# Expert tiles of a routed feed-forward kernel: rows loaded by a transposing DMA, output scatters ahead of the others, longer modelled waits

## The chip, the cores and the metric

The kernel runs on one core of a Trainium2 chip. The metric is the device time of one execution in microseconds (us). Engines are named as in the profile: PE (TensorE matmul), PEld (its weight load), DVE (VectorE), ACT (ScalarE), POOL (GpSimd) and SP (SyncE, which here only issues DMAs).

## The reference

A gated recurrence over four sequences feeds a router with eight experts; each token goes through one expert's two-layer network.

```python
# x, f_logit: (4, 5056, 256); 20224 tokens in all
sig = 1.0 / (1.0 + np.exp(-f_logit))
f = lower_bound + (1.0 - lower_bound) * sig
i = 1.0 - f
for t in range(S):
    h = f[:, t] * h + i[:, t] * x[:, t]
    y[:, t] = h
x = y.reshape(20224, 256)
xn = x / (np.linalg.norm(x, axis=-1, keepdims=True) + 1e-06)
en = expert_emb / (np.linalg.norm(expert_emb, axis=-1, keepdims=True) + 1e-06)
logits = xn @ en.T / tau
expert_idx = np.argmax(logits, axis=1)
probs = softmax(logits)
gate_w = probs[np.arange(N), expert_idx]
for e in range(8):                       # w1: (8, 256, 1024), w2: (8, 1024, 256)
    mask = expert_idx == e
    out[mask] = gate_w[mask, None] * (np.maximum(x[mask] @ w1[e], 0.0) @ w2[e])
```

## The kernel before

The program has two kinds of work. **Chunks**: the 20224 tokens are taken in 40 chunks of 512. For each chunk SP loads `fin` and `xin` (512 KB each, three buffers), PE transposes them (`F_`, line 546, and `X_`, line 575), ACT and DVE make the gates, DVE runs the recurrence as a scan (line 599), PE transposes the result back (`Y_`, line 618) and ACT writes it in bf16 to `Yt`, a row of 256 values per token with the gate weight and the token's number behind them. `route_` and `gate_` work out, for groups of two chunks, each token's expert and its slot `sli`; then POOL scatters the rows, 128 to a DMA, to their slots in `XsScratch`, a table in device memory with a region for each expert (line 832, "an Xs scatter" below; 158 of them, 16 to a batch of four chunks).

**Tiles**: 256 rows of one expert are a tile; there are 86. `tile_` loads the rows to `xsb` (line 996, 132 KB, six buffers), PE transposes them in four pieces into a PSUM bank (`yt`, line 1013), DVE copies them to `ys` (line 1021, two buffers), PE multiplies by the first weights (`mm1`, line 1036, 16 matmuls), ACT and DVE take turns in the four evictions to `hT` (lines 1051 and 1056), PE multiplies by the second weights (`mm2`, line 1067, 16 matmuls), ACT and DVE scale the two halves into `osb` (lines 1081 and 1085, four buffers), and POOL scatters both to the output rows (line 1091, "an output scatter" below, 172 of them). The scale and the output row's number are read from `xsb` too, so a buffer of `xsb` is held until the output scatters that read it are done. For the first 70 tiles `mm1` takes turns in banks 5 and 6 and the transposed rows take bank 5 as well; later tiles have banks of their own.

Which tiles may run is settled by `update_` at eight points, when enough rows of an expert are known; a tile's load waits for the Xs scatters of all groups up to that point.

The order of instructions on each engine is fixed before the run. `Prog.schedule` plays the program through with a cost for each operation, lets each engine take, of what is ready, the operation with the lowest `prio`, and writes the order down; on the chip every engine works through its list in that order, with semaphore waits where data come from elsewhere. `LAT` is the time that the planner adds between an operation and one on another engine that needs it; a DMA takes `DMA_FIX` ns and its bytes over `DMA_RATE`. A tile's `prio` is set in `put`, an Xs scatter's is the number of its chunk:

```python
pr.prio = groups[g][-1] + 3.0 + 0.5 * (j - avail.index((u, g)))
```

Of the kernel before, what the change touches and what calls it, by code (L numbers as in the profile page):

```python
# [7 lines left out]
P = 128  # L8
F32 = mybir.dt.float32
BF16 = mybir.dt.bfloat16  # L10
I32 = mybir.dt.int32
# [5 lines left out]
class Op:  # L17
    __slots__ = (
        "eng", "fn", "deps", "order", "dma", "val", "know", "used", "cost", "nbytes", "prio",
        "idx", "start", "end", "tag",  # L20
    )


class Prog:
# [2 lines left out]

    LAT = 90  # L30
    DMA_FIX = 1900
    DMA_RATE = 300.0

    def __init__(self):
        self.ops = []
# [55 lines left out]
    def schedule(self):  # L91
# [19 lines left out]
        while True:  # L111
# [28 lines left out]
            for q, hard in succ[id(o)]:  # L140
                t = (o.end + self.LAT) if hard else free[e]
                if q.eng == e and o.dma is None and hard:
# [75 lines left out]
def bass_hgrn_recurrence__then__cosine_router_kernel(  # L218
# [12 lines left out]
    E, _, Fdim = moe_w1.shape  # L231
    assert D == 2 * P and Fdim == 8 * P and E == 8 and N % 256 == 0
    DT = D // P
# [4 lines left out]
    NCH = (N + CH - 1) // CH  # L238
    T = 256
    CAP = N + T  # L240
    RW = 264
    NT = N // T + E - 1
    NULLROW = E * CAP
    CB = CAP // T
# [6 lines left out]
    Xs = nc.dram_tensor("XsScratch", [E * CAP + T, RW // 2], I32, kind="Internal").ap()  # L251

    pr = Prog()
    op = pr.op

    with ExitStack() as es:

        def sb(name, shape, dt=F32):
            return es.enter_context(nc.sbuf_tensor(name, shape, dt))
# [7 lines left out]
        identb = sb("identb", [P, P], BF16)  # L267
# [31 lines left out]
        Yt = [sb(f"Yt{q}", [P, 16, RW], BF16) for q in range(NY)]  # L299
# [24 lines left out]
        dac = sb("dac", [P, 2])  # L324
        tbl = [sb(f"tbl{q}", [P, 2], I32) for q in range(NU)]
        nrow = sb("nrow", [P, E], I32)
        NX = 6
        xsb = [sb(f"xsb{q}", [P, 2, RW], BF16) for q in range(NX)]
        ys = [sb(f"ys{q}", [P, DT, T], BF16) for q in range(2)]
        NHT = 2  # L330
        hT = [sb(f"hT{q}", [P, FT, T], BF16) for q in range(NHT)]
        NO = 4
        osb = [sb(f"osb{q}", [P, 2, D]) for q in range(NO)]

        bank = [ps(f"bank{q}", [P, 512]) for q in range(8)]
# [3 lines left out]
        def pool(fn, cost=400, **k):  # L339
            return op("pool", fn, cost, **k)  # L340

        def dve(fn, n, fast=False, **k):
            return op("dve", fn, 130 + n * (0.55 if fast else 1.04), **k)
# [4 lines left out]
        def pe(fn, cost, **k):  # L348
            return op("pe", fn, cost, **k)
# [42 lines left out]
        def iota(dst, pattern, base=0, mult=0, w=()):  # L392
# [7 lines left out]
                out=ident[:], in_=ident[:], compare_op=ALU.not_equal, fill=1.0,  # L400
                base=0, pattern=[[-1, P]], channel_multiplier=1,
            ),
            r=["ident"], w=["ident"],
# [16 lines left out]
                out=scr[:], in_=scr[:], compare_op=ALU.is_ge, fill=1.0,  # L420
                base=0, pattern=[[-1, P]], channel_multiplier=1,
            ),
            r=["scr"], w=["scr"],
# [8 lines left out]
        for q in range(R2):  # L432
            pool(lambda e, q=q: e.memset(exb[q][:], 1e-9), w=[("exb", q)])
        for q in range(NY):
            pool(lambda e, q=q: e.memset(Yt[q][:, :, 260:264], 0.0), w=[("ytz", q)])
        pool(lambda e: e.memset(oh[0][:, 64:72], 0.0), w=[("oh", 0)])

        def late_constants():
# [545 lines left out]
                    )  # L984


        evr = {}

        def tile_(j, u, g, phb, pob, ysb):

            qx, qy, qh, qo = j % NX, j % 2, j % NHT, j % NO
            last = u == len(ups) - 1

            def ld(e):
                r = e.value_load(tbl[u][j : j + 1, 0:1], min_val=0, max_val=NULLROW)
                return e.dma_start(
                    xsb[qx][:].bitcast(I32),
                    Xs[bass.ds(r, T), :].rearrange("(p s) r -> p s r", s=2),
                )

            rd = [("tbl", u), ("nt", 0), ("nt", 1)]
            rd += [("Xs", g_) for g_ in range(g + 1)]
            if last:
                rd += ["nul"]
            op("sp", ld, 700, r=rd, w=[("xsb", qx)], dma=f"xs{qx}", nbytes=135168)

            ysT = bank[ysb][:, 0:256].bitcast(BF16)

            def yt(e):
                o = ysT.rearrange("p (k s c) -> p k s c", k=2, s=2)  # L1010
                for s in range(2):
                    for kt in range(DT):
                        i = e.transpose(  # L1013
                            o[:, kt, s, :], xsb[qx][:, s, kt * P : (kt + 1) * P], identb[:]
                        )
                return i

            pr.prio -= YBOOST
            pe(yt, 310, r=[("xsb", qx), "identb"], x=[ysb])
            dve(  # L1020
                lambda e: e.tensor_copy(ys[qy][:].rearrange("p k c -> p (k c)"), ysT),  # L1021
                512, True, x=[ysb], w=[("ys", qy)],
            )
            pr.prio += YBOOST
            prev = None
            for m in range(4):
                pb = phb[m % len(phb)]

                def mm1(e, m=m, pb=pb):
                    if m == 0:  # L1030
                        evr[j] = e.value_load(
                            tbl[u][j : j + 1, 1:2], min_val=0, max_val=(E - 1) * WE
                        )
                    for fi in range(2):
                        for kt in range(DT):
                            i = e.matmul(  # L1036
                                bank[pb][:, fi * T : (fi + 1) * T],
                                wb[0][:, bass.ds(evr[j] + (kt * Fdim + (2 * m + fi) * P), P)],
                                ys[qy][:, kt, :],
                                start=(kt == 0), stop=(kt == DT - 1),  # L1040
                            )
                    return i

                prev = pe(
                    mm1, 490, r=[("ys", qy), ("tbl", u)] + [("w", i) for i in range(2 * E)],
                    x=[pb], order=[prev],
                )
                o = hT[qh][:, 2 * m : 2 * m + 2, :].rearrange("p f c -> p (f c)")
                if m % 2 == 0:
                    act(  # L1050
                        lambda e, o=o, pb=pb: e.activation(o, bank[pb][:], AF.Relu), 512,  # L1051
                        x=[pb], w=[("hT", qh, m)],
                    )
                else:
                    dve(
                        lambda e, o=o, pb=pb: e.tensor_scalar(  # L1056
                            o, bank[pb][:], 0.0, None, op0=ALU.max
                        ),
                        512, x=[pb], w=[("hT", qh, m)],
                    )  # L1060
            po = [bank[pob[0]][:, 0:D], bank[pob[1]][:, D : 2 * D]]
            one = pob[0] == pob[1]
            for m in range(4):
                def mm2(e, m=m):
                    for kf in (2 * m, 2 * m + 1):
                        for s in range(2):
                            i = e.matmul(  # L1067
                                po[s], hT[qh][:, kf, s * P : (s + 1) * P],
                                wb[1][:, bass.ds(evr[j] + kf * D, D)],
                                start=(kf == 0 and not (one and s)), stop=(kf == FT - 1),  # L1070
                                skip_group_check=one,
                            )
                    return i

                pe(
                    mm2, 480, r=[("hT", qh, m)] + [("w", i) for i in range(2 * E)],
                    x=sorted(set(pob)), order=[prev],
                )
            gx = [xsb[qx][:].bitcast(F32)[:, s, 128:129] for s in range(2)]
            act(  # L1080
                lambda e: e.activation(osb[qo][:, 0, :], po[0], AF.Copy, scale=gx[0]), 256, 1,  # L1081
                x=[pob[0]], r=[("xsb", qx)], w=[("osb", qo, 0)],
            )
            dve(
                lambda e: e.tensor_scalar(osb[qo][:, 1, :], po[1], gx[1], None, op0=ALU.mult),  # L1085
                340, x=[pob[1]], r=[("xsb", qx)], w=[("osb", qo, 1)],
            )
            for s in range(2):
                op(
                    "pool",  # L1090
                    lambda e, s=s: e.indirect_dma_start(  # L1091
                        out=out[:, :],
                        out_offset=bass.IndirectOffsetOnAxis(
                            ap=xsb[qx][:].bitcast(I32)[:, s, 129:130], axis=0
                        ),
                        in_=osb[qo][:, s, :],
                        in_offset=None,
                        bounds_check=N - 1,
                        oob_is_err=False,
                    ),  # L1100
                    1280, r=[("osb", qo, s), ("xsb", qx)], w=[("out", j, s)], dma=f"od{qo}_{s}",
                    nbytes=131072,
                )


# [3 lines left out]
        for u, g in enumerate(ups):  # L1109
            tok = sum(nof(c) for gg in range(g + 1) for c in groups[gg])  # L1110
            k = max(0, -(-(tok - E * (T - 1)) // T)) if u < len(ups) - 1 else NT
# [3 lines left out]
        YBOOST = 1.5  # L1115
# [30 lines left out]
        for j in range(NT):  # L1146
# [3 lines left out]
           r=["nul"])  # L1150
# [38 lines left out]
```

## Time and profile before

| | |
|---|---|
| median of 3 runs | 775.52 us (771.86 to 776.4) |
| the profiled execution | 781.91 us |
| its span, first to last instruction | 780.0 us |
| PE busy | 591.7 us, 76% of the span |
| DVE busy | 399.0 us |
| ACT busy | 342.8 us |
| POOL busy | 387.7 us |
[...]

The spans and durations below are of the profiled execution. Up to 174 us there are chunks alone; from there to about 640 us chunks and tiles share the engines; then tiles alone. Matmul records give the issue times; ends are modelled, so the count of matmuls in a stretch is a better measure of PE's progress than its busy time, above all where the granted clock is low.

### The profile page before, as it was taken

The page shows a single profiled execution, that of the slowest core. Times are in us where ns is not written, and L with a number is a line of the kernel's source. Part 1 is how long each engine was busy: PE and PEld are TensorE (multiplying, and loading weights), DVE is VectorE, ACT ScalarE, POOL GpSimd, SP SyncE. Part 2 cuts the span into 40 slices and gives each one's busy share as a digit, 9 for nine tenths or more (in the row PEclk, how much of TensorE's full clock was granted, in tenths as well). Part 3 has the DMA queues.
Part 4 walks back from the last instruction along what each step waited for, and adds up shares of the span by engine and source line. Part 5 has one row for each costly group of instructions (what it writes and reads, how often), then busy time and mean ns, then how long its engine had stood idle before and what let it go on. Part 6 is the DMA issues. An engine that isn't in the chain of part 4 may idle for free.

```text
span 780.0 us, 14923 instructions
## 1 busy us (share of the span) xinstructions
PE 591.7 (76%) x4656; PEld 430.5 (55%) x4656; DVE 399.0 (51%) x923; ACT 342.8 (44%) x574; POOL 387.7 (50%) x410
## 2 busy tenths in 40 slices
PE   5876676658868996879984698289848866999994
PEld 4543444436556764656763476167535544677773
DVE  4876556616435655354572465157705534445552
ACT  6976556534324623443542265064523522333431
POOL 4267757564644346563347335723572544335443
PEclk9998869769979999999997699579957977999997
DMA  9998886933313424332334244233311113223210
GB/s 277 284 276 209 223 168 195 222 119 106 100 59 104 153 69 134 98 111 84 121 109 136 72 151 127 80 129 123 106 60 56 63 42 117 83 84 99 65 58 1
DMA packets 80534, 95.04 MB, mean 122 GB/s; under 512 B 9089, under 2 KB 70797, under 8 KB 80464
## 3 DMA queue, kind: packets, MB, share of 16 engines
q1 hardware_dynamic: 56592, 54.15, 23.5%
q0 software_dynamic: 23872, 39.94, 18.5%
q8 instruction: 46, 0.75, 0.4%
q14 instruction: 24, 0.20, 0.1%
HBM read 69.83 MB, written 34.44 MB: 134 GB/s over the span
## 4 chain that ended last, share of the span: by engine, by line
PE 61%; another core or an unknown queue 11%; DVE 8%; issue 7%; ACT 7%; POOL 4%; DMA 1%; POOLq 0%; ACTq 0%; DVEq 0%
PE bank L1036 23%; PE bank L1067 19%; PE bank L618 4%; PE bank L546 4%; PE bank L575 3%; PE bank L666 3%; PE bank L1013 3%; POOL XsScratch L832 3%; DVE hb L599 2%; ACT hT L1051 2%; POOL nr L775 2%; DVE hT L1056 2%; DVE nx L583 1%; ACT th L554 1%
## 5 line engine op out<-in xcount | busy, mean ns | idle before, releaser
L1091 POOL DMA_INDIRECT out_dram<-osb,xsb x172 | 171.8, 999 | 257.8 <-DVE osb L1085 162.4
L1036 PE MATMUL bank<-ys,w1b 128*128 128x256 bf16 x1376 | 217.1, 290 | 57.3 <-issue 26.5
L1036 PEld LDWEIGHTS bank<-ys,w1b 128*128 x1376 | 135.5, 99 | 130.8 <-issue 92.0
L832 POOL DMA_INDIRECT XsScratch<-Yt,sli x158 | 164.0, 1038 | 82.9 <-issue 45.4
L1067 PE MATMUL bank<-w2b,hT 128*128 x1376 | 186.1, 282 | 21.2 <-DVE hT L1056 20.8
L1056 DVE TENSOR_SCALAR hT<-bank 128x512 bf16<-128x512 f32 x172 | 118.2, 687 | 90.7 <-PE bank L1036 54.7
L1067 PEld LDWEIGHTS bank<-w2b,hT 128*128 128x128 bf16 x1376 | 131.4, 101 | 43.6 <-issue 24.2
L1051 ACT ACTIVATE hT<-bank 128x512 bf16<-128x512 f32 x172 | 102.4, 596 | 114.5 <-PE bank L1036 87.9
L1081 ACT ACTIVATE osb<-bank,xsb 128x256 f32<-128x256 f32 x86 | 40.7, 473 | 174.2 <-PE bank L1067 104.9
L599 DVE TENSOR_TENSOR_SCAN hb<-fg,hb,nx 128x512 f32<-128x512 f32 (+4 forms) x78 | 97.1, 1245 | 1.4
L1085 DVE TENSOR_SCALAR osb<-bank,xsb 128x256 f32<-128x256 f32 x86 | 41.4, 482 | 103.5 <-ACT osb L1081 82.1
L618 PE MATMUL bank<-ident,hb 128*128 128x128 f32 x316 | 57.3, 311 | 33.4 <-issue 15.2
L546 PE MATMUL bank<-ident,fin 128*128 128x128 f32 x316 | 58.0, 314 | 23.8 <-ACT th L554 10.3
L618 PEld LDWEIGHTS bank<-ident,hb 128*128 128x128 f32 x316 | 40.4, 158 | 54.9 <-issue 33.2
L583 DVE SCALAR_TENSOR_TENSOR nx<-fg,bank 128x512 f32<-128x512 f32 (+1 forms) x80 | 53.9, 673 | 31.6 <-PE bank L575 8.5
L1021 DVE COPY ys<-bank 128x512 bf16<-128x512 bf16 x86 | 36.3, 422 | 64.5 <-issue 16.3
L626 ACT ACTIVATE Yt<-bank 128x512 bf16<-128x512 f32 x79 | 46.6, 590 | 47.9 <-remote 29.2
L560 ACT ACTIVATE fg<-th,cs 128x512 f32<-128x512 f32 (+1 forms) x80 | 64.6, 807 | 1.9
L575 PE MATMUL bank<-ident,xin 128*128 128x128 f32 x316 | 56.6, 308 | 8.9 <-DVE nx L583 8.0
L554 ACT ACTIVATE th<-bank 128x512 f32<-128x512 f32 (+1 forms) x80 | 47.1, 589 | 35.1 <-PE bank L546 20.6
L546 PEld LDWEIGHTS bank<-ident,fin 128*128 128x128 f32 x316 | 42.7, 162 | 28.7 <-ACT th L554 13.9
L611 ACT ACTIVATE sq<-hb 128x1024 f32<-128x1024 f32 (+1 forms) x40 | 41.6, 1041 | 22.4 <-DVE hb L599 21.7
(113 smaller groups left out, 419.7 us busy)
## 6 DMA issues: line engine op xcount, KB each, us to landing
fin<-in_f_logit_dram SPq DMA_DIRECT2D x39, 512.0 KB
xin<-in_x_dram SPq DMA_DIRECT2D x39, 512.0 KB
xsb<-XsScratch SPq DMA_DIRECT2D x86, 132.0 KB
w1b<-in_moe_w_dram POOLq DMA_DIRECT2D x8, 512.0 KB, 7.4
w2b<-in_moe_w_dram POOLq DMA_DIRECT2D x8, 512.0 KB, 7.7
out_dram<-osb,xsb POOLq DMA_INDIRECT x172
XsScratch<-Yt,sli POOLq DMA_INDIRECT x158
XsScratch<-nulr SPq DMA_DIRECT2D x8, 132.0 KB
```

Source lines behind the costliest of these rows:

```text
L546: i = e.transpose(bank[BF][:, b * P : (b + 1) * P], fin[q][:, b, dh * P : (dh + 1) * P], ident[:],)
L560: lambda e, dh=dh: e.activation(fg[c % 2][:, dh, 0:n], th[dh][:, 0:n], AF.Identity, bias=cs[:, dh, 0:1], scale=cs[:, dh, 1:2],),
L575: i = e.transpose(bank[BX][:, b * P : (b + 1) * P], xin[q][:, b, dh * P : (dh + 1) * P], ident[:],)
L583: lambda e, dh=dh: e.scalar_tensor_tensor(out=nx[c % 2][:, dh, 0:n], in0=fg[c % 2][:, dh, 0:n], scalar=1.0, in1=bank[BX][:, 0:n], op0=ALU. ...
L599: lambda e, dh=dh, s0=s0, s1=s1, init=init: e.tensor_tensor_scan(hb[c % NH][:, dh, s0:s1], fg[c % 2][:, dh, s0:s1], nx[c % 2][:, dh, s0:s1 ...
L618: i = e.transpose(bank[BY][:, (b % 2) * D + dh * P : (b % 2) * D + (dh + 1) * P], hb[c % NH][:, dh, b * P : (b + 1) * P], ident[:],)
L832: lambda e, j=o + j, i=o + k_ * 4 + b: e.indirect_dma_start(out=Xs[:, :], out_offset=bass.IndirectOffsetOnAxis(ap=sli[y][:, j : j + 1], axis=0
L1036: i = e.matmul(bank[pb][:, fi * T : (fi + 1) * T], wb[0][:, bass.ds(evr[j] + (kt * Fdim + (2 * m + fi) * P), P)], ys[qy][:, kt, :], start= ...
L1051: lambda e, o=o, pb=pb: e.activation(o, bank[pb][:], AF.Relu), 512,
L1056: lambda e, o=o, pb=pb: e.tensor_scalar(o, bank[pb][:], 0.0, None, op0=ALU.max),
L1067: i = e.matmul(po[s], hT[qh][:, kf, s * P : (s + 1) * P], wb[1][:, bass.ds(evr[j] + kf * D, D)], start=(kf == 0 and not (one and s)), stop ...
L1091: lambda e, s=s: e.indirect_dma_start(out=out[:, :], out_offset=bass.IndirectOffsetOnAxis(ap=xsb[qx][:].bitcast(I32)[:, s, 129:130], axis= ...
```

## The change

The rows of a tile no longer go through PE. SP issues one transposing DMA that reads 256 rows of 512 bytes from `XsScratch` and writes them to `ys` in the layout that `mm1` reads; right behind it a second, plain DMA brings the 8 bytes of each row that hold scale and output row number to a small tile `xm`. `yt`, its PSUM hold and the DVE copy are gone, and `xsb` with them; `ys` has six buffers, `xm` eight. The row of `XsScratch` grows from 528 to 544 bytes. The evictions of the tiles and the output scatters get the priority -1.0, the best there is, and the planner's constants change: 300 ns between engines for 90, and 255 bytes per ns for 300.

```diff
-    LAT = 90
+    LAT = 300
     DMA_FIX = 1900
-    DMA_RATE = 300.0
+    DMA_RATE = 255.0
...
-    RW = 264
+    RW = 272
...
-        NX = 6
-        xsb = [sb(f"xsb{q}", [P, 2, RW], BF16) for q in range(NX)]
-        ys = [sb(f"ys{q}", [P, DT, T], BF16) for q in range(2)]
+        NX = 8
+        xm = [sb(f"xm{q}", [P, 2, 2], I32) for q in range(NX)]
+        NYS = 6
+        ys = [sb(f"ys{q}", [P, DT, T], BF16) for q in range(NYS)]
...
+        EVP = lambda p: -1.0
+        OUTP = lambda p: -1.0
...
             def ld(e):
                 r = e.value_load(tbl[u][j : j + 1, 0:1], min_val=0, max_val=NULLROW)
+                evl[j] = r
+                return e.dma_start_transpose(
+                    ys[qy][:], Xs[bass.ds(r, T), 0:P].bitcast(BF16)
+                )
+
+            def ldm(e):
                 return e.dma_start(
-                    xsb[qx][:].bitcast(I32),
-                    Xs[bass.ds(r, T), :].rearrange("(p s) r -> p s r", s=2),
+                    xm[qx][:],
+                    Xs[bass.ds(evl[j], T), P : P + 2].rearrange("(s p) r -> p s r", p=P),
                 )
...
-            op("sp", ld, 700, r=rd, w=[("xsb", qx)], dma=f"xs{qx}", nbytes=135168)
-
-            ysT = bank[ysb][:, 0:256].bitcast(BF16)
-
-            def yt(e):
-                o = ysT.rearrange("p (k s c) -> p k s c", k=2, s=2)
-                for s in range(2):
-                    for kt in range(DT):
-                        i = e.transpose(
-                            o[:, kt, s, :], xsb[qx][:, s, kt * P : (kt + 1) * P], identb[:]
-                        )
-                return i
-
-            pr.prio -= YBOOST
-            pe(yt, 310, r=[("xsb", qx), "identb"], x=[ysb])
-            dve(
-                lambda e: e.tensor_copy(ys[qy][:].rearrange("p k c -> p (k c)"), ysT),
-                512, True, x=[ysb], w=[("ys", qy)],
-            )
-            pr.prio += YBOOST
+            h = op("sp", ld, 700, r=rd, w=[("ys", qy)], dma=f"xs{qy}", nbytes=135168)
+            op("sp", ldm, 100, r=rd, w=[("xm", qx)], dma=f"xm{qx}", nbytes=16384, order=[h])
...
-                        x=[pb], w=[("hT", qh, m)],
+                        x=[pb], w=[("hT", qh, m)], prio=EVP(pr.prio),
...
-                    1280, r=[("osb", qo, s), ("xsb", qx)], w=[("out", j, s)], dma=f"od{qo}_{s}",
-                    nbytes=131072,
+                    1280, r=[("osb", qo, s), ("xm", qx)], w=[("out", j, s)], dma=f"od{qo}_{s}",
+                    nbytes=131072, prio=OUTP(pr.prio),
```

How the lists of the engines change is shown at three places. The first is POOL's list at the batches of Xs scatters that belong to the chunks from the 25th on; line 832 is an Xs scatter, line 1091 an output scatter, line 775 the square root ahead of a batch's gates. Before:

```order
L1091 DMA out_dram<-osb,xsb 20224x256 x18
L775 TENSOR_TENSOR nr<-nrm,half 128x16
L1091 DMA out_dram<-osb,xsb 20224x256 x2
L832 DMA XsScratch<-Yt,sli 164096x132 x16
L1091 DMA out_dram<-osb,xsb 20224x256 x10
```

The same batch in the changed kernel, where lines have moved by one (833 for 832, 776 for 775) and line 1082 is the output scatter:

```order
L776 TENSOR_TENSOR nr<-nrm,half 128x16
L1082 DMA out_dram<-osb,xm 20224x256 x2
L833 DMA XsScratch<-Yt,sli 164096x136
L1082 DMA out_dram<-osb,xm 20224x256 x2
L833 DMA XsScratch<-Yt,sli 164096x136 x3
L1082 DMA out_dram<-osb,xm 20224x256 x2
L833 DMA XsScratch<-Yt,sli 164096x136 x2
L1082 DMA out_dram<-osb,xm 20224x256 x2
```

The 16 Xs scatters that stood in one piece are now cut by pairs of output scatters into pieces of one to four. So it is for three batches (chunks 25 to 36) and for the short batches of the last four chunks; the two batches ahead of these were cut in this way before as well, and the first four stand in one piece in both kernels.

The second is PE's list at a late tile, from the end of one tile's `mm2` to the start of the next one's `mm1`. Before:

```order
L1067 MATMUL bank<-w2b,hT 128x256 x2
L1013 MATMUL bank<-identb,xsb 128x128 x4
L1031 TENSOR_LOAD tbl
L1031 ISA x2
L1036 ISA
L1036 MATMUL bank<-ys,w1b 128x256
```

And in the changed kernel (line 1058 is `mm2`, line 1027 `mm1`):

```order
L1058 MATMUL bank<-w2b,hT 128x256 x2
L1022 TENSOR_LOAD tbl
L1022 ISA x2
L1027 ISA
L1027 MATMUL bank<-ys,w1b 128x256
```

The four transposes are gone and nothing takes their place. The third is SP's list at one tile's load, before:

```order
L995 TENSOR_LOAD tbl
L995 ISA x2
L996 ISA
L996 DMA xsb<-XsScratch 128x264
```

And in the changed kernel:

```order
L998 TENSOR_LOAD tbl
L998 ISA x2
L1000 ISA
L1000 DMA_TRANSPOSE ys<-XsScratch 128x2x256
L1005 ISA
L1005 DMA xm<-XsScratch 128x2x2
```

One DMA has become two on the same queue. Ahead of the first tile's load stand the `fin` loads of 23 chunks in either list.

## Rows read from the trace of the kernel before

**Rows 1.** The page: span, then PE's busy time, share and instructions.

```profile
span 780.0 us, 14923 instructions
...
PE 591.7 (76%) x4656; PEld 430.5 (55%) x4656; DVE 399.0 (51%) x923; ACT 342.8 (44%) x574; POOL 387.7 (50%) x410
```

**Rows 2.** Busy time by stretch: engines with instruction counts, granted clock, DMA share, GB/s.

```profile
280.00:360.00 80.00, 63.33 (x525) 46.22 (x523) 41.34 (x97) 29.25 (x53) 44.29 (x42) 0.98 0.32 101
360.00:400.00 40.00, 37.45 (x326) 28.79 (x330) 22.93 (x39) 19.60 (x35) 14.71 (x16) 1.00 0.41 127
400.00:440.00 40.00, 22.08 (x161) 15.15 (x162) 15.30 (x49) 12.84 (x23) 23.38 (x22) 0.74 0.28 91
...
480.00:520.00 40.00, 20.98 (x143) 16.62 (x142) 15.88 (x44) 12.86 (x22) 22.02 (x22) 0.66 0.29 87
...
560.00:600.00 40.00, 24.31 (x157) 17.11 (x154) 13.49 (x31) 12.45 (x21) 21.95 (x23) 0.66 0.22 71
600.00:680.00 80.00, 60.17 (x458) 42.95 (x457) 37.78 (x116) 25.71 (x49) 37.34 (x39) 0.87 0.24 75
680.00:760.00 80.00, 78.28 (x660) 59.96 (x659) 40.14 (x74) 29.91 (x54) 35.23 (x36) 1.00 0.25 76
```

**Rows 3.** The same stretches, line 832 alone: POOL busy (count), clock, DMA share, GB/s.

```profile
280.00:360.00 80.00, 16.65 (x16) 0.98 0.32 101
360.00:400.00 40.00, 0.00 (x0) 1.00 0.41 127
...
480.00:520.00 40.00, 15.99 (x16) 0.66 0.29 87
```

**Rows 4.** Timeline from 405 to 445 us: start, duration, instruction, [idle before, releaser].

```profile
410.91 0.96 POOL L832 DMA_INDIRECT XsScratch<-Yt,sli  x1 [0.30 <-DVE val L912]
...
430.11 0.96 POOL L832 DMA_INDIRECT XsScratch<-Yt,sli  x1 [0.30 <-issue]
...
417.73 1.06 PE L618 MATMUL bank<-ident,hb 128*128 128x128 f32 x4
421.69 0.40 PE L1013 MATMUL bank<-identb,xsb 128*128 128x128 bf16 x4 [2.89 <-ACT hT L1051]
...
428.75 1.12 PE L618 MATMUL bank<-ident,hb 128*128 128x128 f32 x4 [5.04 <-issue]
...
435.10 0.42 DVE L1021 COPY ys<-bank 128x512 bf16<-128x512 bf16 x1 [14.82 <-issue]
...
428.10 0.60 ACT L626 ACTIVATE Yt<-bank 128x512 bf16<-128x512 f32 x1 [5.52 <-remote]
```

**Rows 5.** Timeline of DVE in the next such stretch, 478 to 522 us.

```profile
486.40 0.42 DVE L1021 COPY ys<-bank 128x512 bf16<-128x512 bf16 x1 [1.36 <-PE bank L575]
```

**Rows 6.** Timeline from 286 to 302 us, where the two kinds of scatter alternate.

```profile
289.14 1.91 PE L1067 MATMUL bank<-w2b,hT 128*128 x16
...
291.67 0.97 POOL L832 DMA_INDIRECT XsScratch<-Yt,sli  x1 [0.31 <-issue]
...
293.37 0.47 ACT L1081 ACTIVATE osb<-bank,xsb 128x256 f32<-128x256 f32 x1 [4.38 <-PE bank L546]
```

**Rows 7.** Timeline of the last stretch, 722 to 736 us: PE of one tile.

```profile
726.08 2.26 PE L1036 MATMUL bank<-ys,w1b 128*128 128x256 bf16 x16
...
728.28 1.91 PE L1067 MATMUL bank<-w2b,hT 128*128 x16
...
730.02 0.39 PE L1013 MATMUL bank<-identb,xsb 128*128 128x128 bf16 x4
...
730.41 2.18 PE L1036 MATMUL bank<-ys,w1b 128*128 128x256 bf16 x16
```

**Rows 8.** The page's DMA queues: packets, MB, share of 16 engines' span.

```profile
q1 hardware_dynamic: 56592, 54.15, 23.5%
q0 software_dynamic: 23872, 39.94, 18.5%
```

**Rows 9.** Timeline of SP, 120 to 330 us: the first loads of tiles.

```profile
147.28 7.04 SPq L996 DMA_DIRECT2D xsb<-XsScratch  x6
```

More of the change, by code (lines that the diff above doesn't have):

```diff
@@ L19 @@
         "eng", "fn", "deps", "order", "dma", "val", "know", "used", "cost", "nbytes", "prio",
-        "idx", "start", "end", "tag",
+        "idx", "start", "end", "tag", "astart", "aend",
     )
 class Prog:
-    LAT = 90
+    LAT = 300
     DMA_FIX = 1900
-    DMA_RATE = 300.0
+    DMA_RATE = 255.0
     def __init__(self):
@@ L434, in bass_hgrn_recurrence__then__cosine_router_kernel @@
         for q in range(NY):
-            pool(lambda e, q=q: e.memset(Yt[q][:, :, 260:264], 0.0), w=[("ytz", q)])
+            pool(lambda e, q=q: e.memset(Yt[q][:, :, 260:RW], 0.0), w=[("ytz", q)])
         pool(lambda e: e.memset(oh[0][:, 64:72], 0.0), w=[("oh", 0)])
@@ L984, in update_ @@
                     )
-        evr = {}
+        evr, evl = {}, {}
+        EVP = lambda p: -1.0
+        OUTP = lambda p: -1.0
         def tile_(j, u, g, phb, pob, ysb):
-            qx, qy, qh, qo = j % NX, j % 2, j % NHT, j % NO
+            qx, qy, qh, qo = j % NX, j % NYS, j % NHT, j % NO
             last = u == len(ups) - 1
@@ L1058, in tile_ @@
                         ),
-                        512, x=[pb], w=[("hT", qh, m)],
+                        512, x=[pb], w=[("hT", qh, m)], prio=EVP(pr.prio),
                     )
@@ L1078, in tile_ @@
                 )
-            gx = [xsb[qx][:].bitcast(F32)[:, s, 128:129] for s in range(2)]
+            gx = [xm[qx][:].bitcast(F32)[:, s, 0:1] for s in range(2)]
             act(
                 lambda e: e.activation(osb[qo][:, 0, :], po[0], AF.Copy, scale=gx[0]), 256, 1,
-                x=[pob[0]], r=[("xsb", qx)], w=[("osb", qo, 0)],
+                x=[pob[0]], r=[("xm", qx)], w=[("osb", qo, 0)], prio=EVP(pr.prio),
             )
@@ L1085, in tile_ @@
                 lambda e: e.tensor_scalar(osb[qo][:, 1, :], po[1], gx[1], None, op0=ALU.mult),
-                340, x=[pob[1]], r=[("xsb", qx)], w=[("osb", qo, 1)],
+                340, x=[pob[1]], r=[("xm", qx)], w=[("osb", qo, 1)], prio=EVP(pr.prio),
             )
@@ L1093, in tile_ @@
                         out_offset=bass.IndirectOffsetOnAxis(
-                            ap=xsb[qx][:].bitcast(I32)[:, s, 129:130], axis=0
+                            ap=xm[qx][:, s, 1:2], axis=0
                         ),
```

## The prediction

> **What bounds the kernel now.** I read the page first: PE is busy for 76% of the span and no other engine comes near [rows 1]. An average over three kinds of work says little, so next come the stretches. PE's progress is counted in matmul records. From 680 to 760 us, where tiles run alone, it is 660 in 80 us, and from 360 to 400 us, with chunks beside the tiles, 326 in 40 us [rows 2]: together 986 in 120 us, 8.22 per us. This is the pace of an undisturbed stretch, and there PE sets the time. Against it stand three stretches with 161, 143 and 157 records in 40 us, in which the granted clock falls to 0.74 and 0.66 on average because PE sat idle [rows 2]. The 986 - 461 = 525 records that they lack are 525 / 8.22 = 63.9 us, or 21.3 us each. DMA is not the limit there: its share is 0.22 to 0.29, below the 0.41 of the undisturbed stretch [rows 2].
>
> What sets them apart is POOL's work. Stretches with full pace hold no Xs scatter, a slow one holds 16 [rows 3]. The timeline of the first slow one shows how that hurts: the scatters run in one piece from 410.91 to 431.07 us. A transposition of PE that was issued at 417.73 and took 1.06 us is answered by ACT at 428.10; the tile's transposes at 421.69, 0.40 us long, are answered by the DVE copy at 435.10, after an idle time of 14.82 us for which the profile names no cause; PE itself stands for 5.04 us before 428.75 [rows 4]. So results of PE are taken up late while Xs scatters run. Where they alternate with output scatters the delay is still there but ends sooner: `mm2` ends at 289.14 + 1.91 = 291.05, an Xs scatter runs from 291.67 to 292.64, ACT begins at 293.37, 2.3 us late [rows 6]. That stretch, 280 to 360 us, also has 16 Xs scatters [rows 3] and 525 records where 657 would be the pace [rows 2]: 132 / 8.22 = 16.1 us lost. The price of a batch is thus 21.3 us in one piece and 16.1 us cut up. From 600 to 680 us 458 of 657 records are done [rows 2], 24.2 us lost, around the short last batches and the filling of the null rows.
>
> **The change part by part.**
>
> *Cutting the batches.* POOL's list now cuts the three batches that stood in one piece. At the prices above that is 3 x (21.3 - 16.1) = 15.6, say **16 us**. From below, nothing: if the delay goes by the number of scatters, their order changes nothing, and output scatters put ahead make each batch end later. From above, all 64 us, if the cutting together with the removed copy frees PE. I take 16, because 280 to 360 us is the nearest stretch by far: same tiles, same chunks, same 16 scatters. The four batches ahead of the first tile stay in one piece, so the first 174 us stay.
>
> *The transposes.* In the last stretch a tile takes 730.41 - 726.08 = 4.33 us of PE, and between the first transpose at 730.02 and the next `mm1` at 730.41 lie 0.39 us [rows 7]. Some of this is the loading of the table's entry, which stays; I take 0.30 us. In the stretches of rows 2 together, 2430 records in 400 us are 296 us at full pace, so PE sets the time for three quarters: 86 x 0.30 x 0.75 = **19 us**. Bounds: 0, if something else paces the tiles, and 86 x 0.39 = 33 us.
>
> *The copy and its bank.* The copy goes (0.42 us of DVE, hidden beside matmuls) and with it one of six places per tile where another engine takes up a result of PE (transposes, four evictions, the output pair). What is left to lose in the cut batches is 4 x 16.1 + 24.2 = 89 us; a sixth of it is 15, and since such delays overlap I take half, **7 us**. For the first 70 tiles the freed bank 5 lets the first `mm1` group start earlier; I cost that at nothing.
>
> [...] The row shows one copy that waited 14.82 us and began only after the scatters [rows 4], and another that began at 486.40 in the midst of such a batch after 1.36 us [rows 5]. [...]
>
> *The loads.* SP issues two DMAs per tile for one. SP has room: six loads went out in 7.04 us [rows 9], 1.2 us each, where a tile takes 4.33; another half of that per tile, at most, is hidden as long as SP is ahead. It may run ahead by six tiles: `ys` comes free at the end of `mm1` six tiles back, and `xm` at the output scatters of eight tiles back, where `xsb` waited for those of six back. Queued behind a waiting load are the loads of chunks, as before. How long a transposing DMA takes no row shows. Packets are the nearest: 23.5% of 16 x 780 us over 56592 are 52 ns each on q1, 18.5% over 23872 are 97 ns on q0 [rows 8]. A tile needs 256 pieces of 512 bytes or 512 of 256, and 256 of 8 bytes for `xm`: between (256 + 256) x 52 / 16 = 1.7 us and (512 + 256) x 97 / 16 = 4.7 us of all 16 engines. The lower end is hidden under 4.33 us; the upper would add 0.3 us to each of the last 20 or so tiles, 7 us. I take 0, as loads from device memory on this queue have the q1 price. Neither bound excludes that pieces of this kind are dearer than any packet here; that is the second rival.
>
> *Planner's constants, longer rows.* Other constants give other lists of the same work. In the chunk stage the lists differ by single swaps. I take 0, with 10 us to either side. Rows of 544 for 528 bytes are 3% more on a queue with room.
>
> **The sum.** 16 + 19 + 7 = 42 us. The profiled execution took 781.91 us, so 740; the median of the runs shown is 775.52 / 781.91 = 0.992 of it, so **734 us**.
>
> **The rivals.**
>
> *More goes than I count.* If late answers need both a long piece of scatters and the copy in between, the slow stretches come up to full pace: 64 + 33 = 97 us, 685, at 0.992 **679 us**. For it: the longest single waits are the copy's. Against it: 280 to 360 us, cut and yet 16.1 us short. 0.18.
>
> *The transposing loads pace the tiles*, slower than before. All 86 go through one queue in order, the first at 147.28 us [rows 9]; the last tile must be loaded some 15 us before the end. They stretch the run from (782 - 147 - 15) / 86 = 7.2 us per load on; at 8 us it would be 147 + 688 + 15 = 850, at 0.992 **843 us**. Against it: my dear bound is 4.7. For it: nothing here shows the operation. 0.13. [...]
>
> *The change does not do what its order says*: the delay goes by the count of Xs scatters, which stays 158, and PE only reaches the same waits sooner. Then half of the transposes' 19 us is left or nothing: 772 to 782, at 0.992 **766 to 776 us**. 0.14.
>
> **How the numbers follow.** The forecast with its own bounds, some 695 to 760 us, has 0.55. The range of 682 to 774 holds it, nearly all of the third case and half of the first rival; the slow tail stays outside. Below 767.8 us is faster by over 1%, about what a measurement of this kernel can tell from no change: 0.55 + 0.18 + 0.04 = 0.77. Within 1%: 0.10. Slower: 0.13.
>
> **What would show it.** In the profile after: no line for transposes of tiles on PE or the copy on DVE; late tiles about 4.0 us apart; stretches with 16 Xs scatters at 6.6 records per us for 3.8, and no clock below 0.8 there; loads that land before their `mm1` waits. The prediction is wrong if PE waits for transposing loads in the last stretch, if the cut batches cost as much as whole ones, or if undisturbed stretches lose pace.

## The result and the profile after

The kernel after takes 745.45 us (median; 742.42 to 748.41), the kernel before beside it 773.75: a ratio of **0.963**, 95% interval 0.957 to 0.969. The profiled execution took 742.42 us. (In the list of SP, in both kernels, 22 and not 23 `fin` loads stand ahead of the first tile's load.)

The runs of the experiments were made on three chips on which the unchanged kernel before takes 640 to 642 us instead of 774. Which chip the first measurement used is not on record; it is called "the first chip" below, the others "the quiet chips". Every time below stands beside runs of before on its own chip, and the two kernels of the change were run there again.

The page of the kernel after, span, busy time and DMA queues, answers to [rows 1, 8]:

```profile
span 740.6 us, 14362 instructions
...
PE 556.3 (75%) x4312; PEld 408.6 (55%) x4312; DVE 363.8 (49%) x837; ACT 339.3 (46%) x574; POOL 391.2 (53%) x410
...
q1 hardware_dynamic: 114384, 54.01, 28.9%
q0 software_dynamic: 23872, 40.27, 20.5%
```

The span is 39.4 us shorter, which is more than the medians show, 773.75 - 745.45 = 28.3: the profiled execution of before is 8 us over its median, that of after 3 us under. PE's busy time fell by 591.7 - 556.3 = 35.4 us, with 344 matmul records fewer (the transposes, line 1013, were busy for 35.0 us in before). Its idle time is nearly as long as before, 184.3 for 188.3 us. Between the two profiles, then, the gain is for the most part time in which PE no longer works, and hardly any of it is time in which PE no longer waits. Where the idle time lies shows by stretch; first the kernel after, then before (PE busy, granted clock, DMA share, GB/s):

```profile
0.00:174.00 174.00, 108.10 (x736) 0.82 0.83 206
```

```profile
0.00:174.00 174.00, 113.38 (x788) 0.83 0.87 220
```

Up to 174 us PE idles 65.9 us for 60.6, 5.3 more; behind it 118.4 for 127.7, 9.3 less. The stretches that the prediction spoke of, PE first and then line 833 (the Xs scatters) on POOL, in the kernel after:

```profile
280.00:360.00 80.00, 63.45 (x517) 0.96 0.49 126
400.00:480.00 80.00, 64.09 (x538) 0.94 0.52 126
520.00:600.00 80.00, 58.18 (x448) 0.89 0.28 73
```

```profile
280.00:360.00 80.00, 15.54 (x16) 0.96 0.49 126
400.00:480.00 80.00, 17.67 (x17) 0.94 0.52 126
520.00:600.00 80.00, 24.05 (x25) 0.89 0.28 73
```

With 16 and 17 Xs scatters, 517 and 538 records in 80 us are 6.5 and 6.7 per us, and the clock stays above 0.8. The 143 to 161 records in 40 us and the clock of 0.66 to 0.74 in [rows 2] are not their like, as a whole batch fills 40 us and a cut one 80. Of like length in before are the 161 records from 400 to 440 us with those of the 40 us behind it:

```profile
440.00:480.00 40.00, 38.54 (x340) 29.22 (x338) 24.88 (x52) 22.99 (x39) 14.86 (x14) 0.96 0.43 131
```

These are 501 in 80 us, 6.3 per us, and PE idles 19.4 of the 80 us, after the change 15.9 (and from 520 to 600 us, where 25 scatters fall, 21.8). The records of after are 7% fewer for the same work, so they tell a little less than its progress. The cut spreads much of the same loss over a longer time and takes a small part of it away.

Late answers are still there. The idle time of DVE and ACT that the profile can put down to no engine of the program (`remote` and `issue` in the views of waits) adds up to 192.2 us in before and 202.6 in after; only the longest single one fell, from 15.5 to 10.8 us. The timeline of the kernel after around 466 us (start, duration, instruction, [idle before, releaser]):

```profile
462.69 1.47 PE L1058 MATMUL bank<-w2b,hT 128*128 x12
...
465.02 0.96 POOL L833 DMA_INDIRECT XsScratch<-Yt,sli  x1 [0.30 <-issue]
...
467.55 0.96 POOL L833 DMA_INDIRECT XsScratch<-Yt,sli  x1 [0.30 <-issue]
...
470.14 0.69 DVE L1047 TENSOR_SCALAR hT<-bank 128x512 bf16<-128x512 f32 x1 [8.96 <-remote]
...
470.97 1.01 PE L1058 MATMUL bank<-w2b,hT 128*128 x4 [6.80 <-DVE hT L1047]
```

PE ran out at 464.16 and stood 6.80 us for an eviction that DVE began only after three more Xs scatters, with no engine of the program named as its releaser.

Late tiles, which were 4.33 us apart in [rows 7], and SP's loads for the last group, in the kernel after:

```profile
702.13 2.18 PE L1027 MATMUL bank<-ys,w1b 128*128 128x256 bf16 x16
704.25 1.94 PE L1058 MATMUL bank<-w2b,hT 128*128 x16
706.12 2.18 PE L1027 MATMUL bank<-ys,w1b 128*128 128x256 bf16 x16
```

```profile
625.37 1.25 SPq L1000 DMA_TRANSPOSE ys<-XsScratch  x1
626.89 0.34 SPq L1005 DMA_DIRECT2D xm<-XsScratch  x1
627.98 1.21 SPq L1000 DMA_TRANSPOSE ys<-XsScratch  x1
...
638.54 1.21 SPq L1000 DMA_TRANSPOSE ys<-XsScratch  x1
```

The tiles are 3.99 us apart, 0.34 less. SP takes 627.98 - 625.37 = 2.61 us from one tile's loads to the next one's, where [rows 9] had 1.2 for one load.

### The profile page after: what moved, and what is told of

Read it like the earlier page. It is cut to its first block, busy times and chain, and to the rows that moved or that the text cites. A ratio compares the mean times of both kernels' runs of the same rounds, so it can differ in the third digit from the quotient of the medians.

```text
span 740.6 us, 14362 instructions
## 1 busy us (share of the span) xinstructions
PE 556.3 (75%) x4312; PEld 408.6 (55%) x4312; DVE 363.8 (49%) x837; ACT 339.3 (46%) x574; POOL 391.2 (53%) x410
## 3 DMA queue, kind: packets, MB, share of 16 engines
q1 hardware_dynamic: 114384, 54.01, 28.9%
## 5 line engine op out<-in xcount | busy, mean ns | idle before, releaser
L1082 POOL DMA_INDIRECT out_dram<-osb,xm x172 | 177.4, 1032 | 228.3 <-DVE osb L1076 87.9
L1027 PE MATMUL bank<-ys,w1b 128*128 128x256 bf16 x1376 | 209.7, 286 | 63.2 <-ACT hT L1042 34.1
L1058 PE MATMUL bank<-w2b,hT 128*128 x1376 | 179.6, 281 | 31.6 <-DVE hT L1047 16.7
L833 POOL DMA_INDIRECT XsScratch<-Yt,sli x158 | 160.5, 1016 | 63.2 <-issue 45.2
L1058 PEld LDWEIGHTS bank<-w2b,hT 128*128 128x128 bf16 x1376 | 134.1, 100 | 56.2 <-issue 36.5
L1072 ACT ACTIVATE osb<-bank,xm 128x256 f32<-128x256 f32 x86 | 40.6, 472 | 137.1 <-PE bank L1058 62.7
L1076 DVE TENSOR_SCALAR osb<-bank,xm 128x256 f32<-128x256 f32 x86 | 41.4, 481 | 99.6 <-ACT osb L1072 75.9
L547 PE MATMUL bank<-ident,fin 128*128 128x128 f32 x316 | 55.9, 305 | 26.1 <-ACT th L555 16.1
L555 ACT ACTIVATE th<-bank 128x512 f32<-128x512 f32 (+1 forms) x80 | 47.1, 589 | 40.5 <-remote 18.5
L547 PEld LDWEIGHTS bank<-ident,fin 128*128 128x128 f32 x316 | 40.5, 156 | 31.7 <-ACT th L555 20.5
L576 PEld LDWEIGHTS bank<-ident,xin 128*128 128x128 f32 x316 | 42.2, 160 | 17.4 <-DVE nx L584 16.3
```

Of the source, the lines that this page charges most:

```text
L547: i = e.transpose(bank[BF][:, b * P : (b + 1) * P], fin[q][:, b, dh * P : (dh + 1) * P], ident[:],)
L576: i = e.transpose(bank[BX][:, b * P : (b + 1) * P], xin[q][:, b, dh * P : (dh + 1) * P], ident[:],)
L833: lambda e, j=o + j, i=o + k_ * 4 + b: e.indirect_dma_start(out=Xs[:, :], out_offset=bass.IndirectOffsetOnAxis(ap=sli[y][:, j : j + 1], axis=0
L1027: i = e.matmul(bank[pb][:, fi * T : (fi + 1) * T], wb[0][:, bass.ds(evr[j] + (kt * Fdim + (2 * m + fi) * P), P)], ys[qy][:, kt, :], start= ...
L1058: i = e.matmul(po[s], hT[qh][:, kf, s * P : (s + 1) * P], wb[1][:, bass.ds(evr[j] + kf * D, D)], start=(kf == 0 and not (one and s)), stop ...
L1082: lambda e, s=s: e.indirect_dma_start(out=out[:, :], out_offset=bass.IndirectOffsetOnAxis(ap=xm[qx][:, s, 1:2], axis=0), in_=osb[qo][:, s, :],
```

## The experiments

The theories named in the expectations: A is the prediction's (a batch in one piece costs 5 us more than a cut one). B: only the load path counts. C: the long pieces are the whole loss. D: the constants do more than nothing. E: late answers belong to the machine, not to the program. F: the new constants are what makes the load path pay, and the plan takes the loads for too cheap. G, H and K are F's rivals, told where they stand. Times are medians.

**before_again and after_again**: the two kernels, unchanged.

> The kernel before once more, unchanged, for its profile beside the runs of order_cut_alone, costs_alone, load_path_alone and after_old_costs, in which it took 641 us instead of 774. Theory E (late answers are a state of the machine, not of the program): where the time is some 641 us, the stretches with 16 Xs scatters in one piece hold over 280 matmul records in 40 us, and no answer to PE comes over 1 us late; where it is some 774 us they hold about 150. Theory A (late answers belong to these scatters on any chip): about 150 records in both cases.

> The kernel after once more, unchanged. Theory E: where before takes 641 us, there is no loss that cutting the batches could take away; load path alone gave 0.985 and the cut order alone 1.03, so the sum is about 1.00 to 1.03, 641 to 660 us; where before takes 774 us, 0.963 again. Theory A: 0.963 in both cases, 617 us.

Measured: before 642.01 us (the runs of before beside it 640.89), after 618.27, ratio 0.965 (0.963 to 0.968). Theory E holds for the late answers: the idle time of DVE and ACT that no engine of the program ends is 0.7 us in all, 0.5 at the longest; the copy (line 1021) and the eviction to `Yt` (line 626), with 31.8 and 29.2 us of it in before, have none. Stretches of before_again, PE and then line 832, and its timeline inside a batch in one piece:

```profile
400.00:440.00 40.00, 37.87 (x338) 1.00 0.53 160
440.00:480.00 40.00, 37.51 (x342) 1.00 0.33 102
```

```profile
400.00:440.00 40.00, 17.47 (x16) 1.00 0.53 160
440.00:480.00 40.00, 16.32 (x16) 1.00 0.33 102
```

```profile
402.97 0.96 POOL L832 DMA_INDIRECT XsScratch<-Yt,sli  x1 [0.30 <-issue]
...
409.27 0.39 PE L1013 MATMUL bank<-identb,xsb 128*128 128x128 bf16 x4
...
409.69 0.42 DVE L1021 COPY ys<-bank 128x512 bf16<-128x512 bf16 x1 [0.20 <-PE bank L1013]
...
424.06 0.95 POOL L832 DMA_INDIRECT XsScratch<-Yt,sli  x1 [0.30 <-issue]
```

The same batch of 16, in one piece and of much the same pace on POOL (22.0 us for 20.2), and 338 records at a granted clock of 1.00 where [rows 2] have 161. The copy begins 0.03 us after the transposes end, in the midst of the batch; in [rows 4] it begins 435.10 - 422.09 = 13.01 us after them (the 14.82 there are DVE's idle time). But the ratio did not go to 1.00 or above, as E's numbers had it: it is that of the first chip, A's number without A's mechanism. The stretches of both on a quiet chip, before_again, then after_again, with the line of PE from each page:

```profile
0.00:174.00 174.00, 123.98 (x937) 0.91 0.90 232
...
PE 554.2 (87%) x4656; PEld 409.1 (64%) x4656; DVE 396.8 (62%) x923; ACT 342.2 (53%) x574; POOL 392.1 (61%) x410
```

```profile
0.00:174.00 174.00, 115.33 (x860) 0.89 0.90 225
...
PE 519.1 (84%) x4312; PEld 393.7 (64%) x4312; DVE 361.9 (59%) x837; ACT 340.2 (55%) x574; POOL 395.3 (64%) x410
```

PE's busy time falls from 554.2 to 519.1 us, 35.1 less; its idle time grows by 8.7 us up to 174 us (58.7 for 50.0) and by 4.6 behind it (40.5 for 35.9); together 35.1 - 8.7 - 4.6 = 21.8, the difference of the spans, 640.1 and 618.3.

**order_cut_alone**: before, with the output scatters ahead in POOL's order.

```diff
+        OUTP = lambda p: -1.0
...
-                    nbytes=131072,
+                    nbytes=131072, prio=OUTP(pr.prio),
```

> The kernel before, where only the output scatters get the priority -1: POOL's list cuts the three pieces of 16 Xs scatters into pieces of 1 to 5, loads, transposes, copy and costs stay. Theory A (my terms: a batch in one piece costs 5 us more than a cut one, and the load path is worth some 26): 775 - 16 = 759 us, and 400 to 600 us shows no stretch of 40 us below 200 matmul records. Theory B (the order does nothing, the delay goes by the number of Xs scatters; all the gain is the load path's): 772 to 778 us. Theory C (the long pieces are the whole loss): 715 to 735 us.

Measured: 660.4 us beside 641.0, ratio 1.030 (1.025 to 1.035). No theory had it: cutting alone makes the kernel *slower*. (One piece, late in the list, still has nine scatters.) The first and last scatters of one batch and the loads that wait for it, in this run:

```profile
405.22 0.95 POOL L832 DMA_INDIRECT XsScratch<-Yt,sli  x1 [0.30 <-issue]
...
443.07 1.59 POOL L832 DMA_INDIRECT XsScratch<-Yt,sli  x1 [0.30 <-issue]
```

```profile
449.38 5.02 SPq L998 DMA_DIRECT2D xsb<-XsScratch  x5
```

Cut, the batch takes 444.66 - 405.22 = 39.4 us, in one piece in before_again 425.01 - 402.97 = 22.0, and the next loads go out at 449.38 instead of 427.15 (there in the row `427.15 4.04 SPq L996`). From 360 to 520 us PE is busy for 136.8 of 160 us (four stretches of 40 us, the granted clock down to 0.91), in before_again for 144.6. That later loads starve PE is the likely way, but it is shown for a small part of the 19 us only: the waits of PE that the profile puts down to tile loads are 7.6 us here and 5.4 in before_again.

**costs_alone**: before, with the new constants.

```diff
-    LAT = 90
+    LAT = 300
...
-    DMA_RATE = 300.0
+    DMA_RATE = 255.0
```

> The kernel before, where only the planner's constants are the new ones (LAT 300, DMA_RATE 255): all lists are planned anew, and POOL's has no piece over 4 Xs scatters behind the first 64, loads and priorities as before. Theory A: the order cut in this way is worth as much as by priorities, 755 to 765 us. Theory B: 772 to 778 us. Theory D (the longer modelled wait also lets PE's list run ahead of late answers, which no priority does): below 750 us.

Measured: 644.12 us beside 641.0, ratio 1.005 (1.003 to 1.007). The constants alone change next to nothing, B's number. The batches are cut here too, and that one which begins at 384.04 us takes 33.2 us, yet the cut is without its price; what pays for it is not shown. Up to 174 us the run does 864 records, before_again 937.

**load_path_alone**: after, with old constants and without priorities.

```diff
-    LAT = 300
+    LAT = 90
...
-        EVP = lambda p: -1.0
-        OUTP = lambda p: -1.0
+        EVP = lambda p: p
+        OUTP = lambda p: p
```

> The kernel after, with the old constants and without the two priorities: only the transposing load is left of the change, and the three pieces of 16 Xs scatters are back. Theory A: 775 - 26 = 749 us at best, less what the whole pieces keep: 750 to 762 us, and the three stretches with a whole piece stay below 200 matmul records in 40 us. Theory B: 742 to 748 us, as the kernel after, since all of the gain is the load path's. Theory C: 765 to 775 us.

(DMA_RATE 300 as well.) Measured: 630.9 us beside 641.0, ratio 0.985 (0.980 to 0.990). This lies between A's and C's numbers: the load path alone is worth 10 us, though the transposes (line 1013 in before_again) held PE for 33.3. The load path comes as one piece here: that `ys` has six buffers for two, and that the copy and its bank are gone, was not tried apart from the transposes.

**after_old_costs**: after, LAT 90 and DMA_RATE 300 again.

> The kernel after with LAT 90 and DMA_RATE 300 again; the priorities alone cut the batches then (one piece of 9, else up to 5). My prediction put the constants at nothing, 10 us to either side: Theory A 740 to 750 us, as the kernel after. Theory D: slower by over 10 us, 757 or more.

Measured: 657.2 us beside 641.0, ratio 1.025 (1.020 to 1.030), 39 us more than after_again. This is D's case. The run is also 26 us slower than load_path_alone, from which only the priorities set it apart: under the old constants they cost time here, as that of the output scatters alone does in order_cut_alone. About half of the 39 us is seen in the waits of PE's `mm1` for its load (us, times, longest), of this run and of after_again:

```profile
PE bank L1027 <- DMA ys<-XsScratch: 28.0, 5, 7.4
```

```profile
PE bank L1027 <- DMA ys<-XsScratch: 9.2, 1, 9.2
```

**load_and_costs**: after without the two priorities.

```diff
-        EVP = lambda p: -1.0
-        OUTP = lambda p: -1.0
+        EVP = lambda p: p
+        OUTP = lambda p: p
```

> The kernel after without its two priorities: transposing load and new constants. POOL's list is that of after up to the last third, where pieces of 9 and 8 Xs scatters come back. Numbers beside a before of 641 us (where it is 774, times 1.207). Theory F (the constants are what makes the load path pay: they put more loaded tiles ahead of PE, so that a batch that ends late no longer stops it): 613 to 624 us, as after's 618. Theory G (the priorities are needed for it): 628 to 640 us, nearer to the load path alone, 631.

Measured: 616.04 us beside 641.77, ratio 0.960 (0.957 to 0.964). This is F's case; under the new constants the priorities add nothing to the other two parts. The four corners without the priorities on these chips: neither 641, constants 644, load path 631, both 616. The load path is worth 10 us under the old constants and 28 under the new.

**true_load_cost**: after, with SP's real time for a tile's loads as their cost in the plan.

```diff
-            h = op("sp", ld, 700, r=rd, w=[("ys", qy)], dma=f"xs{qy}", nbytes=135168)
-            op("sp", ldm, 100, r=rd, w=[("xm", qx)], dma=f"xm{qx}", nbytes=16384, order=[h])
+            h = op("sp", ld, 1430, r=rd, w=[("ys", qy)], dma=f"xs{qy}", nbytes=135168)
+            op("sp", ldm, 1190, r=rd, w=[("xm", qx)], dma=f"xm{qx}", nbytes=16384, order=[h])
```

> The kernel after, with what SP really takes for a tile's two loads as their costs in the planner (1430 and 1190 ns for 700 and 100; in the trace of after eight tiles follow one another 2.6 us apart). The planner then puts tile 70, whose load is issued sixth of the last group, behind tile 67 instead of behind tile 65. Theory F (the one wait of 9.2 us of PE for a load, at 514 to 523 us, comes from a load that the plan takes to be cheap): 9 us less than after, 609 us beside a before of 641. Theory H (the wait belongs to the last Xs scatters, and PE only stops elsewhere): 616 to 620 us.

Measured: **609.26 us** beside 641.77, ratio 0.950 (0.946 to 0.953), the fastest of these runs, and F's 609. The place in after_again, first PE, then SP:

```profile
513.29 0.68 PE L1027 MATMUL bank<-ys,w1b 128*128 128x256 bf16 x4 [0.28 <-ACT hT L1042]
523.18 1.89 PE L1027 MATMUL bank<-ys,w1b 128*128 128x256 bf16 x8 [9.20 <-DMA ys<-XsScratch]
```

```profile
506.55 1.25 SPq L1000 DMA_TRANSPOSE ys<-XsScratch  x1
...
519.74 1.21 SPq L1000 DMA_TRANSPOSE ys<-XsScratch  x1
```

Tile 70, the first that uses the other banks, stands second of its group on PE and sixth on SP; five loads at 2.64 us lie ahead of its own. With the real costs it stands fourth, and the wait is 2.8 us:

```profile
PE bank L1027 <- DMA ys<-XsScratch: 2.8, 1, 2.8
```

**true_cost_no_prio and load_path_true_cost**: the load costs without the priorities, and with the old constants besides.

> As true_load_cost, without the two priorities. Theory F (with the new constants the priorities are worth nothing or 2 us against, as load_and_costs with 616.0 to after's 618.3): 606 to 611 us. Theory G (the priorities help as soon as the loads are planned right): 613 us or more.

> load_path_alone with the planner's load costs of true_load_cost: old constants, no priorities, whole batches. Theory F (a plan that knows SP's 2.6 us per tile keeps PE from waiting 6 us for tile 70): 620 to 626 us. Theory H (with LAT 90 tiles 49, 57 and 65 wait for the end of their batches, whatever the loads cost in the plan): 628 to 634 us, as the load path alone.

Measured: 611.94 us beside 640.38, ratio 0.956 (0.952 to 0.959), and 623.47, ratio 0.974 (0.968 to 0.980). The second is F's; the first is 1 us over F's range and 1 under G's. Under the new constants the priorities are worth some 3 us at most, and the load path alone gains 7 us more once the plan knows what its loads cost.

**stage_costs**: true_load_cost, with LAT 90 for all that is written ahead of chunk 12.

```diff
-                t = (o.end + self.LAT) if hard else free[e]
+                t = (o.end + (90 if q.idx < self.cut else self.LAT)) if hard else free[e]
```

> As true_load_cost, and the constant LAT is 90 for everything up to chunk 11 and 300 only behind it, so that the first stage keeps the order that it had before. In after and costs_alone this stage does 872 and 878 matmul records in 174 us, before 942. Theory F (the longer modelled wait costs some 8 us in the chunk stage and gains in the tile stage): 600 to 606 us beside a before of 641, over 920 records in the first 174 us. Theory H (the records only come later, what counts is when the Xs scatters end): no gain over true_load_cost, within 3 us.

Measured: 628.23 us beside 641.77, ratio 0.980 (0.974 to 0.985): both theories missed. The first stage is not the old one again but the slowest, 811 records up to 174 us, for 856 in true_load_cost (860, 864 and 937 are the counts of after_again, costs_alone and before_again in one window), and PE's `mm1` waits 14.7 us for loads. The edit gives the first stage its old LAT only: DMA_RATE stays at 255 throughout, and the tiles are planned with 300 from the start. So this is a third order, not the old first stage with the new second one, and what it would take to get that stays open.

**xs_first**: true_load_cost, with the Xs scatters ahead of the output scatters.

```diff
-                            w=[("Xs", g)], dma=f"sc{y}", nbytes=67584, chain=False,
+                            w=[("Xs", g)], dma=f"sc{y}", nbytes=67584, chain=False, prio=-2.0,
```

> As true_load_cost, and Xs scatters get the priority -2, ahead of the output scatters: POOL's list holds five batches of 16 whole, which true_load_cost cuts up; load path, constants and planner's load costs stay. Theory A (of the prediction: a whole batch costs 5 us more than a cut one): 609 + 5 x 5 = 634 us. Theory K (where PE's results are taken up in 0.05 us a whole batch costs nothing, and its earlier end helps the loads behind it): 600 to 609 us beside a before of 641; where before takes 774, theory A.

Measured: 617.18 us beside 640.38, ratio 0.966 (0.961 to 0.971), 8 us over true_load_cost; five whole batches cost 1.6 us each, not A's 5, and K's gain is not there either. PE waits for no tile load now, but longer for evictions; the two costliest of these waits:

```profile
PE bank L1058 <- DVE hT L1047: 4.4, 2, 2.6
PE bank L1027 <- ACT hT L1042: 3.6, 9, 1.1
```

With the waits of `mm1` on DVE they are 10.3 us, in true_load_cost 5.9, while that run's 2.8 for a load are gone. The profiled execution is the fastest of four (614.72 to 620.48), 4 us over that of true_load_cost; what makes the others slower is not shown. So with the new constants a whole and a cut batch are close, and with the old ones the cut costs 19 us.

## Why the prediction was right, step by step

**Sign and size.** 734 was forecast and 745 measured, inside the range; the gain is 28 us by the medians, where 42 were added up. Between the two profiles the sum of 42 comes close to the 39.4 us measured, but its terms do not: 19 us were to come from work taken off PE and 16 + 7 from shorter waits, and PE's busy time fell by 35.4 us and its idle time by 4.0. That the errors cancel is luck, and two of the three terms stand on something that the same program does not show on other chips.

**The transposes: right in kind.** 19 us were taken, with 33 as the bound. PE's busy time fell by 35.4 us on the first chip and 35.1 on a quiet one. Of the two factors that made 19 of 33, 0.30 us a tile is near the 0.34 by which late tiles moved together; the three quarters cannot be told apart from the rest. How much of the work reaches the end depends on what PE waits for instead: on the quiet chips the load path as a whole is worth 10 us under the old constants and 28 under the new, with the 19 between them.

**Cutting the batches: the price is of that machine, and the lower bound was wrong.** The 16 us come from stretches in which answers to PE are late, and on the quiet chips they are not. On the first chip the idle time behind 174 us fell by 9.3 us, on the quiet one it grew by 4.6; these 14 us are the most that is left for terms one and three, 16 + 7. They are assigned by a comparison of chips, not by an edit on the first, and the 8 us by which the profiled execution of before lies over its median are of the same size: a cause argued, not shown. The sum of late answers did not fall with the cut (192.2 and 202.6 us), which speaks against the term and for the third rival's reason, that the delay goes by the number of scatters. That a cut batch ends later was named and bounded with nothing; measured in order_cut_alone, the batch shown takes 17 us longer and the kernel 19, a loss that is gone with the new constants. So the prediction's "from below, nothing" is its failed step.

**The constants: zero was wrong.** They were put at nothing, 10 us to either side. Alone they cost 3 us; with the load path they gain 15 (630.9 to 616.0), and with the load path and the priorities 39 (657.2 to 618.3), as they take away the 26 us that the priorities cost under the old constants: `mm1`'s waits for loads are 28.0 us without them and 9.2 with. They also cost: 77 records less up to 174 us (937 to 860). Of these, 16 are transposes that are gone; the other 61, at (2594 / 306 =) 8.5 per us, the pace of before_again from 174 to 480 us, are an estimated 7 us. On the first chip that stage fell from 788 to 736 records; the prediction's "In the chunk stage the lists differ by single swaps" did not price it.

```profile
174.00:480.00 306.00, 292.48 (x2594) 1.00 0.43 135
```

**The loads: hidden in DMA time as forecast, SP's time wrong.** The dearer packets did not come: q1's share of 16 engines grew from 23.5% of 780.0 to 28.9% of 740.6 us, 214.0 - 183.3 = 30.7 us of all engines for 86 tiles, 0.36 us a tile more than the old loads took; the upper bound of 4.7 us is far off. The price per packet was wrong too, to the good side: at 52 ns the 57792 packets more would have been 188 us. But SP takes 2.6 us for a tile's loads, not 1.8, and a tile that is loaded sixth and used second waits for it: 9.2 us in after_again, and 4.41 at 637.78 us in the recorded run, in a row that names no load but lies behind the sixth, issued at 638.54:

```profile
642.20 1.88 PE L1027 MATMUL bank<-ys,w1b 128*128 128x256 bf16 x8 [4.41 <-issue]
```

True_load_cost gives this back.

**The rivals.** Transposing loads do not pace the tiles: late tiles are 3.99 us apart, and SP is ahead: in 43 waits, 99.2 us, it stands for the `mm1` that frees a tile's buffer. Where nothing holds them up, six tiles' loads follow one another at 2.6 us (the expectation of true_load_cost says eight; the trace has six), and the nine of after_again from 500 to 540 us land 2.7 us after their issue at the median. In DMA time an old load is an estimated 0.46 us of all engines (135 KB at q1's mean in before, 54.15 MB in 183.3 us), and the new pair takes 0.36 more, with the 8-byte pieces of `xm` in it. On SP the six transposing loads of after_again from 506 to 521 us take 1.21 to 1.25 us each, the plain `xm` loads beside them 0.39 to 0.43. That more goes than was counted did not come: with the long pieces and the copy gone, answers are still late on the first chip. That the order does nothing is wrong on the quiet chips, where it cost 19 us; on the first chip no run tells.

**What the prediction said would show.** No transposes or copy, tiles 4.0 us apart (3.99), 6.6 records per us where 16 Xs scatters run (6.5 and 6.7), no clock below 0.8 there (0.87 at the least in any 40 us of them): all seen. But the sign of 6.6 for 3.8 sets 80 us beside 40; over 80 us before had 6.3 already, so this sign says little. "Loads that land before their `mm1` waits": all but that of tile 70.

## What to carry to other kernels

Count the engine time that an edit takes off the bottleneck before any change of stalls: it was 35 us here on either kind of chip, while the stalls came and went with machine and order and left 10 to 28 us of it. Price a re-ordered queue by when its last item lands and who is fed by it, with the loss as the lower end. A planner's costs are part of the kernel: after a load path is changed, put the measured issue time into the plan, which was worth 4 to 9 us for two numbers.

## What the runs showed of the hardware that was not expected

The same program takes 774 us in the first measurement and 641 on three chips later, at much the same instruction durations on POOL and DVE (an Xs scatter 1038 ns in the mean of before and (17.47 + 16.32) / 32 = 1.056 us in the two batches of before_again above, a copy 425 and 425 ns at the median). What differs is the time from a result of PE to its consumer while Xs scatters are issued, 13.01 us in the copy shown against 0.03. In before DVE and ACT have 30 idle times over 2 us that the profile can put down to no engine of the program, and each has Xs scatters in it, 1 to 12. Whether it is the chip, its memory or something beside the program is open; no run of an edit was made where before takes 774. A transposing DMA of 256 rows holds SP for 1.2 us (1.21 to 1.25 in the six of after_again), three times a plain load's 0.36 (`380.50 0.36 SPq L996` in before_again).
